# Attention on one core: TensorE's blocks as one hardware loop, V six pieces behind K, single banks, and queries in 8 KB runs

## Chip, cores, metric

One core of one Trainium2 chip. The metric is the device time of one execution in microseconds. An execution is about 1.8 us longer than the span of its trace (646.7 against 644.9 us before).

## The reference, cut to what matters

```python
B, H, Sq, Skv, Dh = 8, 16, 16, 2048, 256          # bf16
scores = jnp.einsum('bhqd,bhkd->bhqk', q, k) * Dh ** -0.5
attn = softmax(scores, axis=-1)
return jnp.einsum('bhqk,bhkd->bhqd', attn, v)
```

There are 128 heads, each with 1 MB of K and 1 MB of V, and only 16 queries per head. So 268 MB are read once, and little is computed on each byte.

## The kernel before

Work goes in 16 blocks of 8 heads. A block has four pieces of K and four of V, of 2 MB each. For every K piece VectorE transposes it (`kt`, two halves), and TensorE multiplies it with the queries (`qk`) into four PSUM banks, each half as soon as it is transposed. When the four pieces of a block are done, VectorE takes the maximum, ScalarE the exponentials, VectorE transposes the probabilities (`pt`) and spreads them into the weight matrix `PT` (`px`, two halves, written over those of the block before), and TensorE multiplies with V (`pv`, two halves of two pieces each). `evac_a` (ScalarE) and `evac_b` (VectorE) combine and scale the result, and it is stored.

Each engine works through its own list in order, and waits by semaphores. The order of two lists is what this case is about (in shorthand and cut; helpers and the last block's special treatment are left out):

```python
R_KN, R_KB, R_V = 3, 4, 5          # K buffers, transposed half buffers, V buffers

# TensorE
for g in range(G):
    qk(4 * g); qk(4 * g + 1)
    pv(g - 1, 0)
    qk(4 * g + 2); qk(4 * g + 3)
    pv(g - 1, 1)
    qprep(g + 2)                   # transposes of the queries on TensorE

# VectorE
for g in range(G):
    for r in (1, 2, 3):
        kt(4 * g + r, 0); kt(4 * g + r, 1)
    max(g)                         # waits for qk(4g+3)
    kt(4 * g + 4, 0)
    pt(g, 0); pt(g, 1)             # wait for the exponentials
    px(g, 0); px(g, 1)             # wait for the PV before that still reads PT
    ...                            # sum, reciprocal, scale: three small operations
    kt(4 * g + 4, 1)
    evac_b(g - 1)                  # waits for pv(g-1,1) and evac_a

# the load queue (SyncE), in order: K i, then V i-4; queries once behind K 0
QR load: q viewed as "(g p) d -> p g d"     # 2048 rows of 512 B
```

Of the kernel before, what the change touches and what calls it, by code (L numbers as in the profile page):

```python
# [12 lines left out]
R_KN = 3  # L13
R_KB = 4
R_V = 5
# [10 lines left out]
def bass_standalone__softmax_full_bidir__sampling_kernel(  # L26
# [9 lines left out]
    assert SQ == 16 and D == 256 and SKV == 2048 and NH % 8 == 0  # L36
    G = NH // 8
    NP = 4 * G
    scale = float(D) ** -0.5

# [3 lines left out]
    qg = q.rearrange("b h s d -> (b h s) d").rearrange("(g p) d -> p g d", p=128)  # L44

    with ExitStack() as es:
# [4 lines left out]
        QR = ec(nc.sbuf_tensor("QR", [128, G, D], BF16))  # L51
        QW = ec(nc.sbuf_tensor("QW", [128, 2, 2, 8, 128], BF16))
# [15 lines left out]
        XP_ps = ec(nc.psum_tensor("XP_ps", [128, 8, 128], BF16))  # L68
# [8 lines left out]
        def J(eng, cls, emit, deps=(), dma=None):  # L77
            deps = [d for d in deps if d is not None]
            if dma is not None:
                jb = _Job(eng, cls, emit, deps, dma[0], dma[1], 16)  # L80
            else:
                if (eng, cls) not in counters:
                    counters[(eng, cls)] = [ec(nc.semaphore("c_%s_%s" % (eng, cls))), 0]
                c = counters[(eng, cls)]
                c[1] += 1
                jb = _Job(eng, cls, emit, deps, c[0], c[1])
            order[eng].append(jb)
            return jb

        block = ec(nc.Block())  # L90

        KNf = KN[:].bitcast(F32)
# [15 lines left out]
        def emit_qprep(eng, g):  # L108
            qv = QR[:, g, :]
            for bp in range(8):  # L110
                b, par = bp // 2, bp % 2
                for a in range(4):
                    ins = eng.transpose(XP_ps[32 * a:32 * a + 32, bp, :], ap_of(qv, qv.offset + 64 * b + par, [[2, 32]]),  # L113
                                        ident[:], tile_position=(0, 32 * a))
            return ins

        def emit_qwb(eng, g):
            for a in range(4):
                dv = QW[32 * a:32 * a + 32, g % 2, 0, 0, :]
                sv = XP_ps[32 * a:32 * a + 32, 0, :]  # L120
                ins = eng.activation(ap_of(dv, dv.offset + 32 * a, [[8 * 128 + 1, 2], [128, 8], [2, 16]]),  # L121
                                     ap_of(sv, sv.offset + 16 * a, [[64, 2], [128, 8], [1, 16]]),
                                     ACTF.Copy, scale=scale)
            return ins
# [6 lines left out]
        def emit_qk(eng, i, c):  # L131
            g, Gh, half = i // 4, (i % 4) // 2, i % 2
            kb0 = KB[:, (2 * i + c) % R_KB, 0, :]
            for bp in range(8):
                b, par = bp // 2, bp % 2
                ins = eng.matmul(S_ps[:, 2 * half + c, :], QW[:, g % 2, Gh, bp, :],  # L136
                                 ap_of(kb0, kb0.offset + 64 * b + par, [[D, 16], [2, 32]]),
                                 start=(Gh == 0 and bp == 0), stop=(Gh == 1 and bp == 7))
            return ins
# [20 lines left out]
        def emit_pv(eng, g, t0, t1, s0, s1, base):  # L160

            vb = VB[:, 0, 0, :]
            for t in range(t0, t1):
                rhs = ap_of(vb, vb.offset + (s0 * PT_TOK + t - base) * D, [[(s1 - s0) * PT_TOK * D, 2], [1, D]])
                ins = eng.matmul(O_ps[:, g % 2, :], PT[:, t, :], rhs, start=(t == 0), stop=(t == NT - 1))  # L165
            return ins

        def emit_pv1(eng, Gh, t0, t1, buf, base, bank):

            for t in range(t0, t1):  # L170
                ins = eng.matmul(O_ps[:, bank, D * Gh:D * Gh + D], PT[:, t, :], buf[:, t - base, :],  # L171
# [14 lines left out]
        last = G - 1  # L186

        v_of = []
        for j in range(NP):
            g, r = j // 4, j % 4  # L190
            v_of.append((2 * g + r % 2, r // 2) if g < last - 1 else (2 * g + r // 2, r % 2))
        seq = []
        for i in range(NP):
            seq.append(("k", i))
            if i == 0:
                seq.append(("q", 0))
            if 4 <= i < NP - 3:
                seq.append(("v", i - 4))
            elif i == NP - 2:
                seq.append(("v", i - 5))  # L200
        seq += [("v", j) for j in range(NP - 6, NP)]

        j_k, j_v, j_kt, j_qk, j_pv = {}, {}, {}, {}, {}
        j_qwb, j_qprep, j_exp, j_pt, j_px, j_max, j_rab = {}, {}, {}, {}, {}, {}, {}
        j_ea, j_eb, j_st = {}, {}, {}
        tail = {NP - 2: [32], NP - 1: [16, 8, 8]}

        def k_load(i):
            s = i % R_KN
            return J("sp", "ld", lambda eng: eng.dma_start(  # L210
                KN[:, s], ku[i // 2, :, PT_TOK * (i % 2):PT_TOK * (i % 2) + PT_TOK, :]),
                [("kt", i - R_KN, 1) if i >= R_KN else None], dma=(sem_kn[s], 16 * (i // R_KN + 1)))

        def v_buf(j):

            return VB[:, j % R_V] if j < NP - 2 else KN[:, (j - 1) % R_KN]

        def v_load(j, a, n, sem):
            u, h = v_of[j]
            if j < NP - 2:  # L220
                deps = [("pvuse", j - R_V)] if j >= R_V else []
            else:
                deps = [("kt", j - 1, 0), ("kt", j - 1, 1)]
            return J("sp", "ld", lambda eng: eng.dma_start(  # L224
                v_buf(j)[:, a:a + n, :], vu[u, :, PT_TOK * h + a:PT_TOK * h + a + n, :]), deps, dma=sem)

        for what, i in seq:
            if what == "k":
                j_k[i] = k_load(i)
            elif what == "q":  # L230
                j_q = J("sp", "ld", lambda eng: eng.dma_start(QR[:], qg), dma=(sem_q, 16))
            elif i < NP - 2:
                j_v[i] = [v_load(i, 0, PT_TOK, (sem_v[i % R_V], 16 * (i // R_V + 1)))]
            else:
                parts, a = [], 0
                for x, n in enumerate(tail[i]):
                    sem = ec(nc.semaphore("s_vt%d_%d" % (i, x)))
                    parts.append(v_load(i, a, n, (sem, 16)))
                    a += n
                j_v[i] = parts  # L240

        def qprep(g):
            if g < G:
                j_qprep[g] = J("pe", "qprep", lambda eng: emit_qprep(eng, g), [j_q, j_ident, ("qwb", g - 1) if g else None])

        def qwb(g):
            if g < G:
                j_qwb[g] = J("act", "qwb", lambda eng: emit_qwb(eng, g),
                             [("qprep", g), j_qwz, ("qk", 4 * g - 5, 1) if g >= 2 else None])

        def kt(i, h):
            if i < NP:
                j_kt[i, h] = J("dve", "kt", lambda eng: emit_kt(eng, i, h),
                               [j_k[i], ("qk", i - R_KB // 2, h) if i >= R_KB // 2 else None])

        def qk(i):
            if i < NP:
                g = i // 4
                for c in range(2):
                    j_qk[i, c] = J("pe", "qk", lambda eng, c=c: emit_qk(eng, i, c),  # L260
                                   [("kt", i, c), ("qwb", g), ("exp", g - 1, i % 2) if g and i % 4 < 2 else None])

        def pv(g, p):
            if g < 0:
                return
            ja, jb = 4 * g + 2 * p, 4 * g + 2 * p + 1
            j_pv[ja] = j_pv[jb] = J("pe", "pv", lambda eng: emit_pv(
                eng, g, 32 * p, 32 * p + 32, ja % R_V, jb % R_V, 32 * p),
                [("px", g, p), ("eb", g - 2) if g >= 2 else None] + j_v[ja] + j_v[jb])

        def pv_single(j):
            if j < 0:
                return
            g = j // 4
            u, h = v_of[j]
            bank = 2 if g == last and u % 2 else g % 2
            a = 0
            for x, jv in enumerate(j_v[j]):
                n = tail[j][x] if j in tail else PT_TOK
                j_pv[j] = J("pe", "pv", lambda eng, a=a, n=n: emit_pv1(  # L280
                    eng, u % 2, PT_TOK * h + a, PT_TOK * h + a + n, v_buf(j), PT_TOK * h, bank),
                    [("px", g, h), ("eb", g - 2) if g >= 2 else None, jv])
                a += n

        def pt_free(g, h):

            return None if g < 0 else ("pv", 4 * g + 2 * h + 1 if g < last - 1 else 4 * g + 2 + h)

        def softmax_act(g):
            for h in range(2):  # L290
                j_exp[g, h] = J("act", "exp", lambda eng, h=h: emit_exp(eng, g, h),
                                [("max", g), ("pt", g - 1, h) if g else None])

        def evac_a(g):
            if g >= 0:
                dep = ("pv", 4 * g + 1 if g == last else 4 * g + 3)
                j_ea[g] = J("act", "ea", lambda eng: eng.activation(  # L297
                    O_tmp[:], O_ps[:, g % 2, 0:D], ACTF.Copy, scale=rab[:, g, 0:1]),
                    [dep, ("rab", g), ("eb", g - 1) if g else None])

        def evac_b(g):
            if g >= 0:
                dep = ("pv", 4 * g + 3)
# [139 lines left out]
```

## Time and profile before

| | before |
|---|---|
| time, median | 646.8 us (646.6 to 646.9) |
| span of the trace | 644.9 us |
| DMA moved | 270.94 MB |
| GB/s between 60 and 620 us | 428 |
| block period (maximum to maximum, mean of 14) | 39.13 us |

The page of the kernel before: busy time of each engine; then, in 40 slices of the span, the busy share of the DMA engines in tenths and what they moved; then the shares of the chain of waits that ended last.

```profile
PE 515.9 (80%) x2688; PEld 226.4 (35%) x2688; DVE 427.2 (66%) x370; ACT 74.1 (11%) x145; POOL 4.2 (1%) x7
...
DMA  9999999999999999999999999999999999999995
GB/s 341 425 430 426 429 426 430 424 432 426 428 427 428 429 428 428 428 426 429 428 426 431 426 428 428 430 426 427 429 428 427 430 426 429 426 429 429 429 426 209
...
DMA 46%; DVE 33%; PE 16%; issue 4%; SPq 0%
```

The rate is flat at about 428 GB/s from the second slice to the last but one. That says that the stream of K and V is the limit.

The timeline of VectorE of the kernel before, in one block (start, duration, line and operation; in brackets the idle time before it and what ended it):

```profile
289.51 4.50 DVE L128 STREAM_TRANSPOSE KB<-KN 128x2048 f32<-128x2048 f32 x2 [5.43 <-DMA KN<-in_k_dram]
299.31 4.50 DVE L128 STREAM_TRANSPOSE KB<-KN 128x2048 f32<-128x2048 f32 x2 [5.29 <-DMA KN<-in_k_dram]
307.38 2.29 DVE L142 TENSOR_REDUCE negm<-S_ps 128x1 f32<-128x2048 f32 x1 [3.57 <-PE S_ps L136]
...
320.27 0.44 DVE L305 SCALAR_TENSOR_TENSOR O_fin<-O_ps,rab,O_tmp 128x256 bf16<-128x256 f32 x1
320.63 4.49 DVE L128 STREAM_TRANSPOSE KB<-KN 128x2048 f32<-128x2048 f32 x2
328.75 4.50 DVE L128 STREAM_TRANSPOSE KB<-KN 128x2048 f32<-128x2048 f32 x2 [3.63 <-DMA KN<-in_k_dram]
```

K pieces arrive 9.80 us apart (299.31 - 289.51), and VectorE waits for them even shortly after the softmax work of a block. The combine (L305) at 320.27 waits for nothing: the PV that it needs was done. So a block's compute has slack, and DMA sets the pace. The waits of the kernel before say the same (us in total, times, longest):

```profile
DVE KB L128 <- DMA KN<-in_k_dram: 143.2, 35, 6.7
```

### The profile page before, as it was taken

The page shows a single profiled execution, that of the slowest core. Times are in us where ns is not written, and L with a number is a line of the kernel's source. Part 1 is how long each engine was busy: PE and PEld are TensorE (multiplying, and loading weights), DVE is VectorE, ACT ScalarE, POOL GpSimd, SP SyncE. Part 2 cuts the span into 40 slices and gives each one's busy share as a digit, 9 for nine tenths or more (in the row PEclk, how much of TensorE's full clock was granted, in tenths as well). Part 3 has the DMA queues.
Part 4 walks back from the last instruction along what each step waited for, and adds up shares of the span by engine and source line. Part 5 has one row for each costly group of instructions (what it writes and reads, how often), then busy time and mean ns, then how long its engine had stood idle before and what let it go on. Part 6 is the DMA issues. An engine that isn't in the chain of part 4 may idle for free.

```text
span 644.9 us, 6273 instructions
## 1 busy us (share of the span) xinstructions
PE 515.9 (80%) x2688; PEld 226.4 (35%) x2688; DVE 427.2 (66%) x370; ACT 74.1 (11%) x145; POOL 4.2 (1%) x7
## 2 busy tenths in 40 slices
PE   1849887778987779876798787797878797787996
PEld 1314333333333334332343233333323342333575
DVE  3886865857667585765948749477485854957760
ACT  2020200102011020110202002020020200201010
POOL 2000000000000000000000000000000000000000
PEclk9978988898888899887989788988879987899999
DMA  9999999999999999999999999999999999999995
GB/s 341 425 430 426 429 426 430 424 432 426 428 427 428 429 428 428 428 426 429 428 426 431 426 428 428 430 426 427 429 428 427 430 426 429 426 429 429 429 426 209
DMA packets 21580, 270.94 MB, mean 420 GB/s; under 512 B 2352, under 2 KB 4400, under 8 KB 5168
## 3 DMA queue, kind: packets, MB, share of 16 engines
q1 hardware_dynamic: 19248, 269.49, 98.5%
q10 hardware_dynamic: 2304, 1.05, 0.6%
q8 instruction: 21, 0.34, 0.2%
q14 instruction: 7, 0.06, 0.0%
HBM read 269.48 MB, written 1.05 MB: 419 GB/s over the span
## 4 chain that ended last, share of the span: by engine, by line
DMA 46%; DVE 33%; PE 16%; issue 4%; SPq 0%
DMA KN<-in_k_dram 42%; DVE KB L128 17%; PE S_ps L136 14%; DVE PT L157 7%; DVE negm L142 5%; DMA KN<-in_v_dram 4%; DVE PC L151 3%; PE O_ps L171 2%; PE O_ps L165 1%; DVE rinv L361 0%; DVE ltot L359 0%; DVE O_fin L305 0%; DVE rab L362 0%; SPq L224 0%
## 5 line engine op out<-in xcount | busy, mean ns | idle before, releaser
L128 DVE STREAM_TRANSPOSE KB<-KN 128x2048 f32<-128x2048 f32 x128 | 289.4, 2291 | 143.2 <-DMA KN<-in_k_dram 143.2
L136 PE MATMUL S_ps<-KB,QW 128*128 128x512 bf16 x1024 | 287.9, 441 | 109.2 <-DVE KB L128 109.2
L136 PEld LDWEIGHTS S_ps<-KB,QW 128*128 128x128 bf16 x1024 | 106.1, 108 | 282.1 <-DVE KB L128 129.7
L165 PE MATMUL O_ps<-VB,PT 128*128 128x512 bf16 x896 | 197.9, 379 | 0.0
L165 PEld LDWEIGHTS O_ps<-VB,PT 128*128 128x128 bf16 x896 | 87.5, 98 | 105.9
L146 ACT ACTIVATE P_sb<-S_ps,negm 128x1024 bf16<-128x1024 f32 x32 | 35.3, 1109 | 495.8 <-DVE negm L142 495.8
L142 DVE TENSOR_REDUCE negm<-S_ps 128x1 f32<-128x2048 f32 x16 | 36.7, 2292 | 51.9 <-PE S_ps L136 51.9
L157 DVE COPY PT<-PC 32x1024 bf16<-32x1024 bf16 x128 | 52.9, 413 | 1.8
L151 DVE STREAM_TRANSPOSE PC<-P_sb 128x1024 bf16<-128x1024 bf16 x32 | 37.3, 1204 | 1.3 <-ACT P_sb L146 1.3
L121 ACT ACTIVATE QW<-XP_ps 32x256 bf16<-32x256 bf16 x64 | 28.6, 446 | 47.3 <-PE XP_ps L113 46.8
L171 PE MATMUL O_ps<-VB,PT 128*128 128x256 bf16 x192 | 21.8, 272 | 2.0 <-DMA VB<-in_v_dram 2.0
L113 PE MATMUL XP_ps<-ident,QR 128*32 128x128 bf16 x512 | 10.9, 232 | 13.6 <-DMA QR<-in_q_dram 11.7
L171 PEld LDWEIGHTS O_ps<-VB,PT 128*128 128x128 bf16 x192 | 18.6, 98 | 5.3 <-issue 1.5
L305 DVE SCALAR_TENSOR_TENSOR O_fin<-O_ps,rab,O_tmp 128x256 bf16<-128x256 f32 x16 | 7.2, 447 | 14.3 <-PE O_ps L171 14.1
L113 PEld LDWEIGHTS XP_ps<-ident,QR 128*32 128x32 bf16 x512 | 7.9, 102 | 19.8 <-DMA QR<-in_q_dram 11.7
L297 ACT ACTIVATE O_tmp<-O_ps,rab 128x256 f32<-128x256 f32 x16 | 7.6, 473 | 13.8 <-PE O_ps L171 11.2
L171 PE MATMUL O_ps<-KN,PT 128*128 128x256 bf16 x64 | 7.2, 273 | 1.3 <-DMA KN<-in_v_dram 1.3
L171 PEld LDWEIGHTS O_ps<-KN,PT 128*128 128x128 bf16 x64 | 6.2, 98 | 2.2 <-DMA KN<-in_v_dram 1.5
L146 ACT ACTIVATION_READ_ACCUMULATOR P_sb<-S_ps,negm 128x1 f32 x32 | 6.3, 196 | 0.0
L362 DVE TENSOR_SCALAR rab<-mask,rinv 128x2 f32<-128x2 f32 x16 | 3.7, 228 | 0.6
L182 POOL MEMSET PT<- 128x4096 f32 x1 | 3.5, 3511 | 0.0
L361 DVE RECIPROCAL rinv<-ltot 128x1 f32<-128x1 f32 x16 | 2.6, 164 | 0.6
(10 smaller groups left out, 6.6 us busy)
## 6 DMA issues: line engine op xcount, KB each, us to landing
KN<-in_k_dram SPq DMA_DIRECT2D x64, 2048.0 KB, 23.6
VB<-in_v_dram SPq DMA_DIRECT2D x62, 2048.0 KB, 27.8
KN<-in_v_dram SPq DMA_DIRECT2D x1, 2048.0 KB, 27.6
out_dram<-O_fin ACTq DMA_DIRECT2D x16, 64.0 KB, 9.4
KN<-in_v_dram SPq DMA_DIRECT2D x1, 1024.0 KB, 29.6
KN<-in_v_dram SPq DMA_DIRECT2D x2, 512.0 KB, 30.7
QR<-in_q_dram SPq DMA_DIRECT2D x1, 0.5 KB, 10.4
```

Source lines behind the costliest of these rows:

```text
L113: ins = eng.transpose(XP_ps[32 * a:32 * a + 32, bp, :], ap_of(qv, qv.offset + 64 * b + par, [[2, 32]]), ident[:], tile_position=(0, 32 * a))
L121: ins = eng.activation(ap_of(dv, dv.offset + 32 * a, [[8 * 128 + 1, 2], [128, 8], [2, 16]]), ap_of(sv, sv.offset + 16 * a, [[64, 2], [128, ...
L128: return eng.transpose(KBf[:, (2 * i + h) % R_KB].rearrange("p t i -> p (t i)"), KNf[:, i % R_KN].rearrange("p t i -> p (t i)")[:, n * h:n ...
L136: ins = eng.matmul(S_ps[:, 2 * half + c, :], QW[:, g % 2, Gh, bp, :], ap_of(kb0, kb0.offset + 64 * b + par, [[D, 16], [2, 32]]), start=(Gh ...
L142: return eng.tensor_reduce(out=negm[:, g:g + 1], in_=S_ps[:].rearrange("p c n -> p (c n)"), axis=AX.X, op=ALU.max, negate=True)
L146: return eng.activation(P_sb[:, 1024 * h:1024 * h + 1024], S_ps[:, 2 * h:2 * h + 2, :].rearrange("p c n -> p (c n)"), ACTF.Exp, bias=negm[ ...
L151: return eng.transpose(PC[:, h].rearrange("p t x -> p (t x)"), P_sb[:, 1024 * h:1024 * h + 1024])
L157: ins = eng.tensor_copy(PT[pr, 32 * h:32 * h + 32, pr], PC[pr, h])
L165: ins = eng.matmul(O_ps[:, g % 2, :], PT[:, t, :], rhs, start=(t == 0), stop=(t == NT - 1))
L171: ins = eng.matmul(O_ps[:, bank, D * Gh:D * Gh + D], PT[:, t, :], buf[:, t - base, :], start=(t == 0), stop=(t == NT - 1))
L297: j_ea[g] = J("act", "ea", lambda eng: eng.activation(O_tmp[:], O_ps[:, g % 2, 0:D], ACTF.Copy, scale=rab[:, g, 0:1]), [dep, ("rab", g), ( ...
L305: j_eb[g] = J("dve", "eb", lambda eng: eng.scalar_tensor_tensor(out=O_fin[:, g % 2, :], in0=O_ps[:, bank, D:2 * D], scalar=rab[:, g, 1:2], ...
```

## The change

The intent is a smaller program for TensorE: blocks 2 and on become one hardware loop. A loop needs every turn alike, so the last blocks lose their special order, the second banks for query weights and output go, weights are loaded once for two QK matmuls, PV comes two blocks behind QK, and V is loaded six pieces behind K with four V buffers. Queries are loaded in 8 KB runs and transposed on VectorE instead of TensorE. Because one weight load serves both halves of a K piece, a QK now waits for both to be transposed. The diff, cut to its core (the two lists in the shorthand used above, some comments added):

```diff
-R_KN = 3
+R_KN = 4
 R_KB = 4
-R_V = 5
+R_V = 4
+LAG = 6
...
+qx = q... .rearrange("(u a s) d -> a u (s d)", a=4, s=SQ)
+def emit_qload(eng, a):                       # four loads on ScalarE's queue
+    return eng.dma_start(QR[32 * a:32 * a + 2 * G, :], qx[a])
...
+            for c in range(2):                # emit_qk: one weight load, two matmuls
+                mm = eng.matmul if c == 0 else (lambda *x, **y: mm_kept(eng, *x, **y))
...
+        for i in range(NP + LAG):
+            if i < NP:
+                k_load(i)
+            if i >= LAG:
+                v_load(i - LAG)   # V piece 4g, 4g+1 wait for pv(g-1,0); 4g+2, 4g+3 for pv(g-1,1)
...
 # TensorE
-            qk(4 * g); qk(4 * g + 1); pv(g - 1, 0); qk(4 * g + 2); qk(4 * g + 3); pv(g - 1, 1); qprep(g + 2)
+            pv(g - 2, 0)
+            qk(4 * g)
+            qk(4 * g + 1)
+            pv(g - 2, 1)
+            qk(4 * g + 2)
+            qk(4 * g + 3)
...
 # VectorE
+        for g in range(G + 1):
+            max(g - 1)
+            kt(4 * g)
+            pt(g - 1, 0); pt(g - 1, 1)
+            px(g - 1, 0)
+            ...                               # sum, reciprocal, scale
+            kt(4 * g + 1)
+            kt(4 * g + 2)
+            evac_b(g - 2)
+            px(g - 1, 1)
+            kt(4 * g + 3)
...
+            with nc.Fori(0, STEP * len(turns), STEP, ..., head_slot={eng.engine: 0}) as it:
+                ...                           # six jobs a turn; waits against a register
```

## The prediction

> What bounds the kernel now. The page shows a span of 644.9 us, the DMA engines at 99% in every slice but the first and last, 426 to 430 GB/s, 270.9 MB. The table of stretches gives a DMA share of 1.00 from 60 to 620 us. TensorE is at 80%, VectorE at 66%. So the kernel is limited by the K and V stream: one pair of 2 MB pieces per 9.8 us (K transposes at 289.51 and 299.31 us), 39.2 us per block of four pairs. The rest is about 3 us of start and 8 us of end. In the timeline the compute of one block has a slack of several us: VectorE still waits for K (143 us in total in the waits).
>
> What the change does.
> - Queries: 2048 packets of 512 B become 8 KB runs. Before, they delayed K piece 1 by 8.5 - 4.9 = 3.6 us; 1 MB at 428 GB/s is 2.4 us. Gain about 1 us, once. 512 small TensorE matmuls go (10.9 us busy, off the critical path).
> - Loop on TensorE: saves about 0.2 MB of instruction fetch (0.5 us of DMA at most). The body has about 240 instructions. [...]
> - Kept weights: 512 weight loads less; matmuls of 512 columns stay at 0.228 us (warm) or 0.428 us (cold).
> - Order and single buffers. This is what I expect to matter. VectorE now does, per block: maximum, K transpose 0, two P transposes, spread half 0, K transposes 1 and 2, final combine of two blocks back, spread half 1, K transpose 3. The combine and spread 1 wait for the second PV product, which on TensorE stands behind QK of piece 1. That closes a serial ring from one maximum to the next. With durations of the timeline: maximum 2.3 + K transpose 4.5 + P transposes 2.3 + spread 1.7 + small ops 0.6 + K transpose 4.5 + QK + PV 7.1 + scaled copy 0.5 + combine 0.5 + spread 1.7 + K transpose 4.5 + QK, with hand-over about 30.4 us and two QK pieces. QK is 3.65 us warm. Ahead of them TensorE idles about 5.1 and 3.6 us; in this trace gaps of 2.4 to 5.2 us were followed by QK of 5.3 to 6.5 us at the low clock. So 41 to 42 us per block with both cold, 39.7 with one, 37.7 with none. DMA needs 39.2. The compute ring, not DMA, becomes the bound; the 5 us of slack in the V ring are eaten within three blocks.
>
> Sum: first two blocks end about 64.5 us; 14 blocks at 41.3 are 578; the end (two PV of 7.1, four of 3.6, combine and store 2.9) 31.5; outside the span 1.9. Total 676 us, range 652 to 692.
>
> Chances: faster by over 2% 0.04, within 2% 0.12, slower 0.84.
>
> What would show it: the chain of waits shows DVE and PE in place of DMA; mean DMA share falls to about 94% with gaps once or twice a block; V loads wait for PV in the DMA queue's waits; VectorE waits for PE at the combine; K transposes hardly wait for DMA; block period by the maxima 41 us instead of 39.3. Queries land before 10 us. Instruction packets fall from 28 to about 15.
>
> What would make it wrong: TensorE stays warm in both QK pieces; then the ring is 37.7 us, DMA stays the bound, and the time is about 643. [...]

Two passages about the fetching of instructions are cut, a rule with what was concluded from it and one way of being wrong: no trace or run of this case shows what they rested on. The 0.2 MB of instruction fetch is an estimate; the pages show 0.40 MB before and 0.13 MB after. Where the prediction has 0.228 and 0.428 us for a matmul, the starts of matmuls are 0.216 and 0.427 us apart in both traces (medians).

## The result, and the profile after

| | before | after |
|---|---|---|
| time, median | 646.8 us | 679.0 us (678.2 to 681.5, 4 runs) |
| span of the profiled run | 644.9 us | 679.7 us |
| ratio | | 1.0505 (1.0477 to 1.0533) |
| block period, mean of 14 | 39.13 us | 40.97 us |
| GB/s in the blocks | 428 | 407 |
| first maximum begins at | 34.25 us | 43.94 us |
| from the last maximum to the end | 27.6 us | 30.7 us |

Ratios are the mean time of one kernel's fast runs over that of the other's of the same rounds, so not quite the ratio of the medians. The profiled run was the slowest of the four; its trace is explained here.

Where the 34.8 us of the spans went: the beginning of the second maximum moved from 69.50 to 75.47 us (6.0 us), the 14 blocks after it grew from 547.8 to 573.5 us (25.7 us), and the end from 27.6 to 30.7 us (3.1 us).

The page of the kernel after, the same lines, and the line of the instruction queue q8 (21 packets and 0.34 MB before):

```profile
PE 508.8 (75%) x2112; PEld 162.1 (24%) x1600; DVE 426.2 (63%) x371; ACT 99.7 (15%) x209; POOL 4.2 (1%) x7
...
DMA  9999999999999999999999999999999999999693
GB/s 239 422 430 431 402 415 419 413 387 428 410 413 401 411 409 412 425 395 425 398 412 416 424 399 417 400 428 396 433 401 408 406 410 421 420 390 431 281 424 127
...
q8 instruction: 4, 0.07, 0.0%
...
DVE 48%; PE 43%; issue 4%; DMA 2%; ACT 1%; ACTq 0%; DVEq 0%
```

Neither VectorE nor TensorE does more work than before: the busy time of the first is the same and that of the second is less (ScalarE's grows from 74 to 100 us, 15% of the span). But the chain that ended last has DMA at 2% where it had 46%, and VectorE and TensorE share the rest. The rate is now uneven, 387 to 431 GB/s in most slices. The row of DMA shares hides it up to the last slices. The table of stretches gives it as numbers. A line has the stretch, its length, the busy time of PE, PEld, DVE, ACT and POOL with the number of instructions, and then three means: the clock granted to TensorE (1 is full speed), the DMA share and GB/s. First the kernel before, then the kernel after:

```profile
60.00:620.00 560.00, 462.83 (x2311) 196.36 (x2310) 378.55 (x325) 62.41 (x123) 0.00 (x0) 0.90 1.01 428
```

```profile
76.00:649.00 573.00, 445.93 (x1793) 136.67 (x1346) 369.32 (x323) 83.89 (x177) 0.00 (x0) 0.87 0.98 407
```

The share fell by 3%, the rate by 5%.

The timeline of VectorE of the kernel after, one whole block from maximum to maximum:

```profile
321.32 2.29 DVE L154 TENSOR_REDUCE negm<-S_ps 128x1 f32<-128x2048 f32 x1 [5.42 <-PE S_ps L136]
323.52 4.49 DVE L131 STREAM_TRANSPOSE KB<-KN 128x2048 f32<-128x2048 f32 x2
327.94 2.33 DVE L163 STREAM_TRANSPOSE PC<-P_sb 128x1024 bf16<-128x1024 bf16 x2
330.20 1.67 DVE L169 COPY PT<-PC 32x1024 bf16<-32x1024 bf16 x4
...
332.42 8.88 DVE L131 STREAM_TRANSPOSE KB<-KN 128x2048 f32<-128x2048 f32 x4
350.22 0.48 DVE L292 SCALAR_TENSOR_TENSOR O_fin<-O_ps,rab,O_tmp 128x256 bf16<-128x256 f32 x1 [8.91 <-ACT O_tmp L285]
350.62 1.70 DVE L169 COPY PT<-PC 32x1024 bf16<-32x1024 bf16 x4
352.35 4.50 DVE L131 STREAM_TRANSPOSE KB<-KN 128x2048 f32<-128x2048 f32 x2
362.27 2.29 DVE L154 TENSOR_REDUCE negm<-S_ps 128x1 f32<-128x2048 f32 x1 [5.42 <-PE S_ps L136]
```

No transpose of K waits for DMA any more. VectorE waits twice, in the end both times for TensorE: 8.91 us at the combine (the bracket names the scaled copy on ScalarE, which itself waits for PV) and 5.42 us at the maximum. TensorE's lines of the same block fill these waits. The first is the first QK matmul of K piece 1, then a matmul in the middle of that QK, then the second PV, and then the same for QK of piece 3, with the first PV of the next block behind it:

```profile
336.98 0.61 PE L149 MATMUL S_ps<-KB,QW 128*128 128x512 bf16 x1 [5.19 <-DVE KB L131]
...
340.37 0.63 PE L149 MATMUL S_ps<-KB,QW 128*128 128x512 bf16 x1
...
342.44 7.07 PE L177 MATMUL O_ps<-VB,PT 128*128 128x512 bf16 x32
...
356.91 0.39 PE L149 MATMUL S_ps<-KB,QW 128*128 128x512 bf16 x1 [3.94 <-DVE KB L131]
...
358.76 0.63 PE L136 MATMUL S_ps<-KB,QW 128*128 128x512 bf16 x1
...
362.07 4.26 PE L177 MATMUL O_ps<-VB,PT 128*128 128x512 bf16 x19
```

Read the two lists together and the ring closes: a chain in which each step waits for the one before, from one maximum to the next. VectorE works without a pause from 321.32 on, and has transposed K piece 1 at 336.9 (it goes on with piece 2 until 341.3). Then QK 1 (5.5 us), PV (6.9), the scaled copy on ScalarE and the combine (1.3), the spread (1.7), K transpose 3 (4.5), QK 3 (5.2), and the next maximum. That QK 1 and QK 3 wait for both halves of a piece lengthens this ring too; no run here tells by how much. A record of 0.63 us is a matmul at the low clock, one of 0.38 us at the full one; their starts are 0.43 and 0.22 us apart. The granted clock is 0.50 from 334.22 to 341.04 and from 358.11 to 361.52 us, and 1.00 between and right after these stretches. Both QKs begin after an idle gap (5.19 and 3.94 us) and run partly at the low clock.

The load queue shows the same from the other side. Its waits, before and after (the line of the K load waits for the transposes that free the K buffers, the line of the V load for PV):

```profile
SPq L210 <- DVE KB L128: 525.2, 61, 16.5
...
SPq L224 <- PE O_ps L165: 15.5, 9, 5.4
```

```profile
SPq L232 <- PE O_ps L177: 522.0, 28, 20.0
SPq L213 <- DVE KB L131: 57.2, 7, 22.0
```

A queue that waits is not itself a loss: it waited for 525 us in the kernel before too, while the loads already issued kept DMA busy. What changed is whom it waits for.

A turn of the loop costs nothing that the trace shows. At the turn the last QK matmul began 0.21 us before the first PV matmul (361.86 and 362.07), as between any two matmuls. Instruction packets fell from 28 to 11 (0.40 to 0.13 MB). Only the entry into the loop shows: before the first PV of block 2's turn TensorE stands still for 1.20 us without a wait that the profile names.

```profile
76.63 7.07 PE L177 MATMUL O_ps<-VB,PT 128*128 128x512 bf16 x32 [1.20 <-issue]
```

All nine traces with the loop have such a gap there, of 1.1 to 3.1 us, once; the four with the loop written out (runs 1, 5, 10 and 12) have none. Why is not shown. The body is about 240 instructions, and no stall is seen at a turn; no run here has a longer body, so what one would cost is not shown.

### The profile page after: what moved, and what is told of

Same layout as the page of the kernel before. It is cut to its first block, busy times and chain, and to the rows that moved or that the text cites. A ratio compares the mean times of both kernels' runs of the same rounds, so it can differ in the third digit from the quotient of the medians.

```text
span 679.7 us, 4771 instructions
## 1 busy us (share of the span) xinstructions
PE 508.8 (75%) x2112; PEld 162.1 (24%) x1600; DVE 426.2 (63%) x371; ACT 99.7 (15%) x209; POOL 4.2 (1%) x7
## 4 chain that ended last, share of the span: by engine, by line
DVE 48%; PE 43%; issue 4%; DMA 2%; ACT 1%; ACTq 0%; DVEq 0%
DVE KB L131 31%; PE O_ps L177 16%; PE S_ps L149 13%; PE S_ps L136 12%; DVE PT L169 7%; DVE negm L154 5%; DVE PC L163 3%; DMA VB<-in_q_dram 2%; PE O_ps L183 2%; ACT O_tmp L285 1%; DVE O_fin L292 0%; DVE rinv L342 0%; DVE ltot L339 0%; DVE QT L118 0%; ACTq L115 0%
## 5 line engine op out<-in xcount | busy, mean ns | idle before, releaser
L149 PE MATMUL S_ps<-KB,QW 128*128 128x512 bf16 x512 | 228.8, 447 | 166.7 <-DVE KB L131 166.7
L131 DVE STREAM_TRANSPOSE KB<-KN 128x2048 f32<-128x2048 f32 x128 | 286.0, 2282 | 2.6 <-PE S_ps L136 2.2
L136 PE MATMUL S_ps<-KB,QW 128*128 128x512 bf16 x512 | 226.5, 442 | 0.0
L177 PE MATMUL O_ps<-VB,PT 128*128 128x512 bf16 x960 | 211.8, 379 | 1.2 <-issue 1.2
L149 PEld LDWEIGHTS S_ps<-KB,QW 128*128 128x128 bf16 x512 | 56.0, 109 | 390.8 <-issue 193.7
L177 PEld LDWEIGHTS O_ps<-VB,PT 128*128 128x128 bf16 x960 | 93.6, 98 | 121.9 <-issue 12.0
L124 ACT ACTIVATE QW<-QT 32x128 bf16<-32x128 bf16 x128 | 54.0, 422 | 436.3 <-PE S_ps L136 419.0
L163 DVE STREAM_TRANSPOSE PC<-P_sb 128x1024 bf16<-128x1024 bf16 x32 | 37.3, 1203 | 1.3 <-ACT P_sb L158 1.3
L183 PE MATMUL O_ps<-KN,PT 128*128 128x256 bf16 x128 | 14.1, 273 | 0.0
L183 PEld LDWEIGHTS O_ps<-KN,PT 128*128 128x128 bf16 x128 | 12.5, 98 | 1.7
L118 DVE STREAM_TRANSPOSE QT<-VB 128x2048 f32<-128x2048 f32 x1 | 2.3, 2311 | 16.0 <-DMA VB<-in_q_dram 16.0
L339 DVE TENSOR_REDUCE ltot<-lsum 128x1 f32<-128x2 f32 x16 | 2.5, 155 | 0.5
```

Source lines behind the costliest of these rows:

```text
L124: ins = eng.activation(ap_of(dv, dv.offset + 32 * a + e, [[256, 4], [128, 2], [2, 16]]), ap_of(sv, sv.offset + 2 * (2 * g + e), [[64, 4], ...
L131: return eng.transpose(KBf[:, (2 * i + h) % R_KB].rearrange("p t i -> p (t i)"), KNf[:, i % R_KN].rearrange("p t i -> p (t i)")[:, n * h:n ...
L136: return eng.add_instruction(mybir.InstMatmult(start_tensor_calc=start, stop_tensor_calc=stop, ldweights=False, tile_size=(128, 128), tile ...
L149: ins = mm(S_ps[:, 2 * half + c, :], QW[:, e, bp, :], rhs, start=(e == 0 and bp == 0), stop=(e == 1 and bp == 7))
L163: return eng.transpose(PC[:, h].rearrange("p t x -> p (t x)"), P_sb[:, 1024 * h:1024 * h + 1024])
L177: ins = eng.matmul(O_ps[:, 0, :], PT[:, t, :], rhs, start=(t == 0), stop=(t == NT - 1))
```

## The experiments

Twelve kernels were run, four on one chip each time, with the kernel before among them (646.8 to 646.9 us each time). All twelve are recorded as correct, also run 9, whose queries lie on the wrong partitions: the inputs are so small (0.05 times a normal value) that, by an estimate from the reference, the scores differ by about 0.0025 and all weights of the softmax are nearly equal. So the check says little about queries and K here.

### 1. The loop written out

```diff
-            emit_pe(eng)                # the loop
+            emit_stream(eng, "pe")      # the same order of jobs, constant waits
```

> The changed kernel with TensorE's loop written out again (constant waits), the order of jobs as it is. Theory (a serial ring of VectorE and TensorE sets 40.95 us per block, the loop costs nothing): 679 us within 2, block period 40.95 us. Rival (the loop's branch, register waits or refetch cost the time): back to about 647, period near 39.3.

Measured: 678.7 us (678.1 to 679.5), ratio 1.0496; block period 40.95 to 40.97 us. The loop is neither the cost nor a gain in time, within the spread of the runs. Instruction packets rose to 22.

### 2. VectorE's order: spread 1 behind K transpose 3

```diff
+            kt(4 * g + 3)
             evac_b(g - 2)
             px(g - 1, 1)
-            kt(4 * g + 3)
```

> VectorE does K transpose 3 before the combine and spread 1, everything else as changed. Theory: the second PV leaves the ring, which falls to 36 to 38 us, DMA (39.2 us per block) binds again, about 646 us (643 to 652); VectorE waits for K, the V loads wait little. Rival (loop, kept weights, LAG 6 or the single banks as such): 675 to 681.

Measured: 652.5 us (650.6 to 653.4), ratio 1.0092. The blocks take 39.1 us (mean of 14) and the chain that ended last has DMA at 45% again:

```profile
DMA 45%; PE 35%; DVE 13%; issue 6%; SPq 1%; ACTq 0%; DVEq 0%
```

26 of the 32 us are gone with one line moved.

### 3. TensorE's order: the second PV ahead of QK 1

```diff
             pv(g - 2, 0)
             qk(4 * g)
-            qk(4 * g + 1)
             pv(g - 2, 1)
+            qk(4 * g + 1)
             qk(4 * g + 2)
```

> TensorE does the second PV before QK of piece 1 in place of after it; VectorE's order as changed. Theory: the ring loses one QK and the wait for it, about 31 us, DMA binds, the same time as the run with the late spread within 2 us, about 646 (643 to 652). Rival: 675 to 681. If only VectorE's order mattered, this run would stay at 679.

Measured: 652.1 us (651.1 to 653.7), ratio 1.0076; blocks of 39.0 us, and DMA leads the chain:

```profile
DMA 64%; PE 25%; DVE 7%; issue 2%; SPq 2%; ACT 0%; ACTq 0%; DVEq 0%
```

Runs 2 and 3 change different engines, and have in common only that they cut the ring: each gives the same time, within 0.5 us. Both lie just above the range that was expected (643 to 652), since the slow start (next run) is still in them: the rate dips to 381 and 346 GB/s in slice 6, where the first V loads wait for the late first PVs.

### 4. Queries first on K's queue

```diff
-j_q = [J("act", "ldq", ...)]
+j_q = [J("sp", "ldq", ...)]     # ahead of K 0 in the same queue
```

> The four query loads go ahead of K piece 0 on the same DMA queue, nothing else. In the changed kernel queries landed at 18 us, K and queries together moved only 266 GB/s until then, and the first QK began at 24.8. Theory (while compute binds, every us of the start counts): first QK near 15 to 16 us, total 669 to 673, block period still 40.95. If the slow start were hidden behind DMA: 679 still. If 8 KB runs are slow by themselves the queries alone will take over 4 us.

Why: in the kernel after, the transpose of the queries, which everything waits for, shows when they landed:

```profile
18.05 2.31 DVE L118 STREAM_TRANSPOSE QT<-VB 128x2048 f32<-128x2048 f32 x1 [15.98 <-DMA VB<-in_q_dram]
```

Measured: 674.8 us (670.8 to 675.7), ratio 1.042, a miss by 2 us of the expected time: about 4 to 5 us were gained. Queries landed at 7.8 us, the first QK began at 17.1, the first maximum at 36.4 instead of 43.9. From the fourth maximum on the period is 40.95 to 40.97 us again. Between the two profiled runs the first maximum came 7.5 us earlier and the last one 7.4 us: the start counts in full while compute binds. The medians differ by only 4.2 us; the profiled run of the kernel after was its slowest, and the start varies (in the trace of run 1, with the same order of jobs and loads, the first maximum began at 41.50 us and not at 43.94). The queries are slow even at the head of the queue: from 2 to 8 us the rate was 262 GB/s, with K 0 behind them.

### 5. TensorE kept busy in the gaps

```diff
+            for _ in range({0: 18, 2: 12}.get(i % 4, 0) if 4 <= i else 0):
+                ins = mm_kept(eng, W_ps[:], QW[:, e, 7, :], QT[:, 0:512], True, True)   # result unused
```

> The changed kernel, loop written out, with idle-filling matmuls into a spare PSUM bank: 18 behind QK of piece 0 and 12 behind QK of piece 2 of every block but the first (results unused). They add about 6.5 us of TensorE work per block in gaps that were idle, so the gaps shrink from 5.2 and 3.9 us to about 1.3 us. Theory (the low clock after the gaps is part of the ring, twice about 2 us): QK stays at 3.5 us, the ring falls from 40.95 to about 37.5 us, DMA (39.2) binds, 650 to 656 us. Rival (the ring is only order and durations, the clock a bystander, or the extra work costs time): 679 or more.

Measured: 649.7 us (649.2 to 650.5), ratio 1.0044, just under the expected range. This kernel does 450 matmuls more than its twin of run 1 and is 29 us faster. The table of stretches shows the clock at 0.98 where it was 0.87, and the full DMA rate:

```profile
100.00:600.00 500.00, 452.17 (x2036) 119.84 (x1229) 342.68 (x298) 78.45 (x165) 0.00 (x0) 0.98 1.01 428
```

Until compute had caught up with DMA after the late start, four blocks in a row took 37.23 to 37.30 us: that is the ring with both QKs at the full clock (granted clock 1.00 from 74 to 223 us), which the prediction had put at 37.7. The last ten blocks average 39.3 us, and in them VectorE waits for K again (59 us from 223 us on, its largest wait). So the low clock in two QKs (about 3.7 us per block) is what lifts the ring above DMA's 39.2 us.

### 6. and 7. Is the period a sum, or locked?

From the fourth block on, every block of the kernel after took 40.91 to 40.97 us, which is steadier than a chain over three engines has reason to be. The clock record of its trace consists of 62 stretches of 1.00 or 0.50, and their starts all lie on one grid of 3.413 us (a straight line through them misses none by more than 0.001 us); the 53 stretches of the kernel before lie on such a grid too. The low stretches last one or two steps (3.41 or 6.83 us; the first of the kernel before lasts 13.65, and the last of the kernel after is cut off by the end of the record), and from 54.32 to 648.24 us the clock of the kernel after rises to 1.00 every 20.48 us, six steps. Twelve steps are 40.96 us; this is the grid that the expectations below speak of. The matmuls show the same: the change to the full clock within QK falls at 320.68, 341.14 and 361.64 us, 20.46 and 20.50 us apart. Two runs change the length of the ring a little.

```diff
 # run 6: sum and reciprocal done twice, 0.4 us more in the ring
+for rep in range(2):
     js = J("dve", "sm", ... tensor_reduce ...)
     jr = J("dve", "sm", ... reciprocal ...)
 # run 7: sum, reciprocal and scale moved behind kt(4g+3), 0.62 us less
```

> Two small VectorE operations (sum and reciprocal, about 0.4 us together) are done twice in the ring of the changed kernel. Theory A (the block period of 40.95 us is locked to the steps of the TensorE clock, whose changes lie on a grid of 3.413 us; 12 of these are 40.96): the period stays 40.95 and the time within 2 us of 679. Theory B (the period is just the sum of the ring): period 41.35, time 679 + 14 x 0.4 = 684 to 685.

> The three small VectorE operations (0.62 us) go behind K transpose 3 but before the maximum... in the order of the stream, so they move to a place where VectorE waits for QK of piece 3, off the ring. Theory A (locked period): 40.95 still, or a jump to another set of grid steps, time 679 within 2 if locked. Theory B: period 40.33, time about 670.

Measured for run 6: 682.2 us (681.4 to 684.2), between the two expectations, but the period decides. The maxima of its last blocks, VectorE's timeline:

```profile
567.75 2.29 DVE L154 TENSOR_REDUCE negm<-S_ps 128x1 f32<-128x2048 f32 x1 [5.42 <-PE S_ps L136]
608.70 2.29 DVE L154 TENSOR_REDUCE negm<-S_ps 128x1 f32<-128x2048 f32 x1 [5.41 <-PE S_ps L136]
649.67 2.29 DVE L154 TENSOR_REDUCE negm<-S_ps 128x1 f32<-128x2048 f32 x1 [5.42 <-PE S_ps L136]
```

40.95 and 40.97 us, not 41.35 (the nine last blocks are all 40.95 to 40.97). The 0.4 us per block vanished; the extra time came with the second block after the start, which took 44.87 us instead of 41.39.

Measured for run 7: 675.7 us with a wide spread (669.9 to 678.6), so its times don't separate the theories. Its maxima do:

```profile
521.25 2.29 DVE L154 TENSOR_REDUCE negm<-S_ps 128x1 f32<-128x2048 f32 x1 [5.68 <-PE S_ps L136]
561.76 2.29 DVE L154 TENSOR_REDUCE negm<-S_ps 128x1 f32<-128x2048 f32 x1 [4.91 <-PE S_ps L136]
603.22 2.29 DVE L154 TENSOR_REDUCE negm<-S_ps 128x1 f32<-128x2048 f32 x1 [5.64 <-PE S_ps L136]
643.72 2.29 DVE L154 TENSOR_REDUCE negm<-S_ps 128x1 f32<-128x2048 f32 x1 [4.92 <-PE S_ps L136]
```

Blocks alternate between 40.5 and 41.4 us. Two of them are 81.96 us here (643.72 - 561.76), and 24 steps of the grid are 81.92. The mean of the last eleven blocks is 40.91, not 40.33. So in these traces the ring is locked to the grid on which the clock changes, and a small change of it moves the period not at all, or hardly.

How the 0.4 us vanish stands in run 6's trace. QK of piece 1 and the PV behind it:

```profile
338.02 0.61 PE L149 MATMUL S_ps<-KB,QW 128*128 128x512 bf16 x1 [5.57 <-DVE KB L131]
...
343.10 7.07 PE L177 MATMUL O_ps<-VB,PT 128*128 128x512 bf16 x32
```

The idle gap before QK 1 grew from 5.19 to 5.57 us, and QK 1 shrank from 5.46 (336.98 to 342.44 in the kernel after) to 5.08 us. The full clock came 3.35 us after its start (at 341.37) instead of 4.16 us (at 341.14). So the QK that started 0.38 us later in the ring spent 0.81 us less of itself at the low clock, was 0.38 us shorter, and gave back what was added. In run 7 QK 1 starts after a shorter gap (4.67 us), and from 330 to 480 us QK 1 and QK 3 together take 10.7 and 11.6 us in turn, where the kernel after has 10.6.

Each kernel has one trace, so it is not shown that every execution locks: the fastest of run 7, 669.9 us, is what theory B says.

### 8. V four pieces behind K instead of six

```diff
-LAG = 6
+LAG = 4
```

> V four pieces behind K in place of six, nothing else. My theory of the queue: with the V ring of four, V piece 4g waits for the first PV of a block, and with a distance of 4 the K pieces 4g+5 and 4g+7, which the ring needs in that same block, stand behind such waiting V loads in the one DMA queue; the block then grows to about 57 us (the loads of a V and a K, 11.8 us, twice in the ring): 850 to 920 us. So the distance of six is no cost but what lets four V buffers suffice. Rival (the distance is part of the loss): 645 to 670.

Measured, one run: 941.5 us, blocks of 59.6 us (mean of 14), above the range but by the mechanism expected: waits of VectorE for K, none in the kernel after, are now 323 us.

```profile
DVE KB L131 <- DMA KN<-in_k_dram: 323.1, 42, 10.6
```

The distance of six is no part of the loss (run 11 below keeps it and is as fast as the kernel before). With four V buffers a distance of four is too short, because the K loads stand in one queue behind V loads that wait for PV (786.7 us in 28 waits). The 11.8 us in the expectation is the author's estimate. Two pieces at the pace of the kernel before are 9.8 us; K 0 there was issued at 0.73 us and landed at 8.14, 2.5 us more than one piece at that pace.

### 9. Queries in one load of 128 rows (on the wrong partitions, on purpose)

```diff
-j_q = [J("act", "ldq", lambda eng, a=a: emit_qload(eng, a), ...) for a in range(4)]
+j_q = [J("act", "ldq", lambda eng: eng.dma_start(QR, q... .rearrange("(p s) d -> p (s d)", s=SQ)), ...)]
```

> Wrong result on purpose: the 1 MB of queries is read by one load of 128 rows of 8 KB in the order of memory (so heads lie on the wrong partitions), still on the ACT queue beside K. Theory (each of the four loads fills only 32 partitions, and that is what is slow and holds K back): queries land by 10 us, over 380 GB/s in the first 17 us, first maximum near 36, total 671 to 676. Rival (two queues that share the DMA engines are slow, whatever the rows): landing at 16 to 18 us, total 679.

Measured: 674.6 us (671.3 to 676.6), ratio 1.0424. Queries landed at 10.95 us instead of 18.05, the first maximum began at 36.8. The stretch from 4 to 17 us, first in the kernel after, then in this run (last column GB/s):

```profile
4.00:17.00 13.00, 0.00 (x0) 0.00 (x0) 0.00 (x0) 0.23 (x1) 0.92 (x1) 1.00 1.01 263
```

```profile
4.00:17.00 13.00, 0.00 (x0) 0.00 (x0) 6.05 (x3) 3.40 (x8) 0.92 (x1) 1.00 1.01 433
```

The rows are 8 KB in both, and the second queue is used in both, so neither is enough by itself to make it slow. What is left is four loads of 32 partitions each, whose rows lie 32 KB apart in memory, against one load of 128 partitions from consecutive memory; this run changes all three, and doesn't tell them apart. Note the DMA share: 1.01 in both stretches.

### 10. Weights loaded before every QK matmul

```diff
-                mm = eng.matmul if c == 0 else (lambda *x, **y: mm_kept(eng, *x, **y))
+                mm = eng.matmul         # loop written out
```

> Loop written out and the weights loaded again before every QK matmul (512 weight loads more). Theory: weight loads overlap the matmul before, so the block period stays 40.95 and the time 678 to 680, as with the loop alone written out. Rival (kept weights save time): over 684.

Measured: 679.4 us (677.9 to 680.1), ratio 1.0497; the same as run 1. Kept weights save 512 weight loads and no time. Loads run beside matmuls in this trace: from 100 to 600 us it shows 386.9 us of matmuls and 158.6 us of weight loads, 545 us of work in 500. The wait for both halves of a K piece, which came with them, is still in this run.

### 11. and 12. Towards a version that beats both

Run 11 joins runs 3 and 4. Run 12 adds, with the loop written out, a PV of V piece 56 and 20 filling matmuls ahead of the last QK.

```diff
 # run 12, beyond runs 3 and 4
             qk(4 * g + 2)
+            if g == last:
+                pv_single(0, 0)         # V piece 56 alone, then 20 matmuls without use
             qk(4 * g + 3)
```

> Second PV before QK 1 and queries ahead of K 0. Theory: no ring, no start loss: K 0 lands at 12.6, then one piece per 4.9 us, the last V at about 635, end 638.5 in the span, 640 to 642 us: about 1% under the kernel before. If the losses of the two parts did not add up: 647 to 652.

> Second PV before QK 1, queries first, loop written out, and at the end the PV of V piece 56 (with 20 filling matmuls) goes ahead of the last QK, so TensorE has 3.6 us less to do behind it and meets it warm (1.5 us). In the run without this the DMA traffic was over at about 637 and TensorE worked until 642. Expected end of the span 640.5 to 642, time 642 to 644, 0.4 to 0.7% under the kernel before.

Measured: 647.0 us (646.8 to 647.7), ratio 1.0003, and 646.6 us (646.5 to 646.6), ratio 0.9996 (0.9982 to 1.0010). Both are the kernel before again, and no better. So the ring and the start together are the whole loss: run 11 keeps the loop, the kept weights, the distance of six and the single banks. Its chain:

```profile
DMA 69%; PE 21%; DVE 6%; SPq 2%; issue 2%; DVEq 0%
```

Against the expectations both are misses. In run 11 the last K piece landed at 604.5 us and not at about 600 (120 pieces of 4.9 us behind K 0), and TensorE worked until 642.2 while the DMA rate was down to 94 GB/s from 636 us on. In run 12 the filling matmuls ran until 613.7 us although the last K transpose was done at 609.5, so they delayed what they should help. A version that beats the kernel before by a clear margin was not found.

## Why the prediction was right, and where its terms were off

- **The bound moves from DMA to a ring of VectorE and TensorE: right.** The prediction gave 41.3 us per block from the old trace's durations; measured 40.97 (mean of 14). Runs 2 and 3 cut the ring at two places, and each brings the blocks back to 39 us.
- **Both QKs at the low clock: right, and shown by run 5.** The warm ring was put at 37.7 us; run 5 shows 37.2 to 37.3. What the prediction did not see is that the period locks to the grid of the clock's changes (runs 6 and 7): 40.96 is 12 steps of 3.413 us, and changes of the ring by half a microsecond hardly show in it.
- **"Queries land before 10 us", "gain about 1 us": wrong.** They landed at 18.05 us, and the rate until then was 263 GB/s. This is the mis-sized term of the sum: "first two blocks end about 64.5 us" measured 75.5. It cost 11 us against the sum in the profiled run (7 us in the trace of run 1, where the same maximum is at 71.4); with the queries first it is at 66.2. Run 4 gives back about 4 us of time and 7.4 us of its profiled span, run 9 about 4 us.
- **The sum held because two errors cancelled in part.** The start was 11.0 us over, the 14 blocks 4.7 us under (573.5 for 14 times 41.3, 578.2), the end 0.8 us under (30.7 for 31.5). 676 was predicted; the profiled run took 681.5, and the median is 679.0. That the total came so close is in part luck.
- **The loop, the kept weights and the instruction fetch cost or save next to nothing: right** (runs 1 and 10). A turn costs nothing that is seen, the entry once 1.2 us.
- **"Mean DMA share falls to about 94%": wrong as worded.** The share is 0.98; it is the rate that fell, to 407 of 428 GB/s, which is 95%. The sign to watch was GB/s.
- **"V loads wait for PV", "VectorE waits for PE at the combine", "K transposes hardly wait for DMA": right.** 522 us, 129 us and none.

## What to carry to other kernels

When a list of jobs is reordered to make every turn of a loop alike, follow one turn from an operation to its next occurrence through all engines' lists, and add up the durations: here neither VectorE nor TensorE became busier, and 26 of the 32 us were lost because one wait of VectorE was placed behind one PV that stood behind one QK. Compare the sum with the pace of the stream that has to bind, and count matmuls after idle gaps at the low clock (here 0.43 us apart until it rose, then 0.22). For a DMA-bound kernel read GB/s and not the busy share (1.01 here at both 263 and 433 GB/s), and look at the first microseconds by themselves.
